# Attention scores in PSUM: one four-bank tile for two key tiles, in place of two double-bank tiles

## The chip, the cores and the metric

The kernel runs on one core of a Trainium2 chip. The metric is the device time of one execution in microseconds (us); the kernel before took 431.75 us (median of 3 runs, 431.55 to 432.01). The engines are TensorE (PE; its weight loads are PEld), VectorE (DVE), ScalarE (ACT), GpSimd (POOL) and SyncE (SP), which issues the DMAs.

## The reference, cut to what matters

```python
# q, k, v: (2, 12, 448, 64)
scores = q @ k.T / sqrt(64)
attn = softmax(cap * tanh(scores / cap))            # cap = 30
x = (attn @ v) as (2, 448, 768)
h = gelu(x @ w_in)                                  # 768 -> 1024
u, v = h[..., :512], h[..., 512:]
v = layernorm(v) * g_ln
x = x + (u * (w_sg @ v + b_sg)) @ w_out             # w_sg mixes the 448 positions
u = x + (relu(x.T @ w_tok1) @ w_tok2).T             # 448 -> 256 -> 448
out = u + relu(u @ w_ch1) @ w_ch2                   # 768 -> 1536 -> 768
```

Matrices other than the attention weights are split into a high and a low part (`hi`, `lo`), and a product is three matmuls: hi·hi, hi·lo, lo·hi.

## The kernel before, in words

Attention goes over 12 pairs of heads (`attention_all`). A pair has 448 keys: three key tiles of 128 (`j` = 0, 1, 2) with both heads, and a last tile that holds the 64 remaining keys of both heads. For each key tile PE writes the scores, keys by queries, into a PSUM tile `sc` of two banks, one bank per head (`scores`, matmuls of L574; the last tile `last`, L694, fills one bank). ACT takes the tanh from PSUM into an SBUF tile (L548) and then the exp in place (L556), both in `weigh`. The next step multiplies by the values (`values`, L611, four-byte floats, two records of the trace for each matmul; `rest_of`, L594, for the last key tile) into two banks `A` from the tag `gm`, and DVE normalises (`normalise`).

PSUM has eight banks: four single banks (`gm`) and two double banks (`sc`). `sc` also serves the transposes (`tr_unit`, L948) and the first layer of the channel MLP (`ch1_unit`). SBUF tiles come from tags with a fixed number of buffers (`BUFS`).

The order of work on each engine is written by a planner (`Plan.schedule`), not by hand. It takes the operations with estimated durations and keys, and each time it issues the operation that can start first on its engine; of those that can start at once, the one with the lowest key. A dependency between engines costs `LAT` = 140 ns in the plan. A buffer of a tag is handed out in the order of keys: an operation can only take one when all tiles of its tag with lower keys can have theirs too. The order that comes out is fixed; on the chip each engine works through its own list.

In step `n` the keys say: scores of key tiles 0 and 1 of pair `n` (key 10n, one PE operation of 12 matmuls; for `n` = 0 two operations of 6), the values of key tiles 0 and 1 of pair `n-1` (10n + 0.5, four operations of one matmul), scores of key tile 2 together with the rest of pair `n-1` (10n + 4), the last key tile (10n + 4.1), the values of key tile 2 of pair `n-1` (10n + 5, two operations). From the sixth pair on, matmuls of the first MLP for batch 0 (L305) are ready too and can lie between them. Beside the attention, weights are read, rebuilt from 8-byte floats and split: ACT L430, L441, L454; DVE L461, L472, L483; the split L382, L386, L398, L399. The query and key tiles of a pair are split too (tag `q`, DVE L398 for the low part).

After the attention: the first MLP of batch 1 (136 to 167 us), the mixing over positions `sg_unit` (to 185), `out_unit`, the transposes (202 to 224), `tok1_unit`, `tok2_unit` (234 to 249), `ch1_unit` (249 to 336) and `ch2_unit` (336 to 423).

Of the kernel before, what the change touches and what calls it, by code (L numbers as in the profile page):

```python
# [8 lines left out]
F32R = mybir.dt.float32r  # L9
# [235 lines left out]
class Net:  # L245
# [79 lines left out]
    def consts(self):  # L325
        nc, io = self.nc, self.io
        c = lambda name, shape, dt=F32: self.pool.tile(shape, dt, tag=name, name=name, bufs=1)
        cap = c("cap", [128, 1])
        self.acap = c("acap", [128, 1])
        self.qs = c("qs", [128, 1])  # L330
        self.guard = c("guard", [128, 1])
        self.cb = Buf("const", None, None)
        self.cb.ap = cap
        self.gb = Buf("const", None, None)
        self.gb.ap = self.guard
        self.load(512, lambda: nc.sync.dma_start(out=cap, in_=io["cap"]), [self.cb], key=-14.85)
# [32 lines left out]
        warm = self.bank2()  # L369
# [173 lines left out]
    def weigh(self, sc, nn, te, key, dt=0.2):  # L543

        nc = self.nc
        self.act(
            nn * S,
            lambda: nc.scalar.activation(te.ap, sc[:, 0:nn, :S], AF.Tanh, scale=self.qs),  # L548
            [sc, self.cb],
            [te],  # L550
            60,
            key,
        )
        self.last_exp = self.exps[int(key // 10)] = self.act(
            nn * S,
            lambda: nc.scalar.activation(te.ap, te.ap, AF.Exp, scale=self.acap),  # L556
            [te, self.cb],
            [te],
            190,
            key + dt,  # L560
        )

    def scores(self, qk, js, key, more=(), extra=0.0):

        nc = self.nc
        part, tiles = qk[:2]
        scs = [self.bank2() for _ in js]

        def fn():
            for sc, j in zip(scs, js):  # L570
# [9 lines left out]
        self.pe(  # L580
            3 * len(js) + 3.7 * len(more) + 0.5,
            fn,
            (tiles if js[0] else tiles[:2]) + [t for m in more for t in m[1]],
            scs + [t for m in more for t in m[2]],
            key,
        )
        return scs

    def rest_of(self, qk, E, A):


        def fn():
            for h, rows in enumerate((LO, UP)):
                self.nc.tensor.matmul(  # L594
                    A[h][:, :S],
                    qk[2][rows, 9:11].rearrange("p c d -> p (c d)"),
                    E[3][rows, 0],
                    start=False,
                    stop=False,
                )  # L600

        return fn, [qk[2], E[3]], A

    def values(self, qk, E, A, js, key):
        nc = self.nc
        V = qk[2]
        for j in js:
            for h in range(2):

                def av(j=j, h=h):  # L610
                    nc.tensor.matmul(  # L611
                        A[h][:, :S],
                        V[:, 3 * j + h : 3 * j + h + 2].rearrange("p c d -> p (c d)"),
                        E[j][:, h],
                        start=(j == 0),
                        stop=(j == 2),
                    )

                self.pe(3.7, av, [V, E[j]], [A[h]], key)

    def normalise(self, n, A):
        nc = self.nc
# [44 lines left out]
    def attention_all(self):  # L667
# [3 lines left out]
        for n in range(B * NP + 1):  # L671
            k0 = 10.0 * n
            if n < B * NP:
                qk = self.pair_in(n)
                E = {j: self.a([128, 2, S]) for j in range(3)}
                E[3] = self.h([128, 1, S])
                A = [self.bank() for _ in range(2)]
                for js in ([[0], [1]] if n == 0 else [[0, 1]]):
                    for i, (j, sc) in enumerate(zip(js, self.scores(qk, js, k0 + 0.3 * js[0]))):
                        self.weigh(sc, 2, E[j], k0 + 0.1 * j)  # L680
            if old:
                oqk, oE, oA = old
                self.values(oqk, oE, oA, [0, 1], k0 + 0.5)
                more = [self.rest_of(oqk, oE, oA)]
            if n < B * NP:
                (sc,) = self.scores(qk, [2], k0 + 4, more if old else ())
                self.weigh(sc, 2, E[2], k0 + 4)
                sc = self.bank2()

                def last(sc=sc, part=qk[0]):  # L690

                    ks, every = slice(KJ[3], KJ[3] + 128), slice(0, 128)
                    for t, (k, q) in enumerate(THREE):
                        nc.tensor.matmul(sc[:, 0, :S], part(k, every, ks), part(q, every, QC), start=(t == 0), stop=(t == 2))  # L694

                self.pe(3.5, last, qk[1], [sc], k0 + 4.1)
                self.weigh(sc, 1, E[3], k0 + 4.1)
            else:
                f, r, w = more[0]
                self.pe(4, f, r, w, k0 + 4)  # L700
# [1 line left out]
                self.values(oqk, oE, oA, [2], k0 + 5)  # L702
                xs.append(self.normalise(n - 1, oA))
            if n < B * NP:
                old = qk, E, A
        return xs

    def attention_anycap(self, n):
# [231 lines left out]
    def tr_unit(self, x2, s):  # L940

        nc = self.nc
        ps = self.bank2()
        cs = slice(0, 128) if s is None else slice(s * 128, (s + 1) * 128)

        def fn():
            for d in range(ND):
                nc.tensor.transpose(ps[:, d // 3, (d % 3) * 128 : (d % 3 + 1) * 128], x2[d][:, cs], self.ident)  # L948

        self.pe(3, fn, x2, [ps])  # L950
        t = [self.a([128, 2, 384], F32R) for _ in range(2)]
        src = lambda p=slice(0, 128): ps[p, :, 0:384]
        if s is None:
            self.halves(768, lambda b, p: t[b][p], src, [ps], t, True)
        else:
            hi, lo = t
            self.act(768, lambda: nc.scalar.copy(hi.ap, src()), [ps], [hi], 50)
            self.rest(768, lambda: lo.ap, src, lambda: hi.ap, [ps, hi], [lo], psum=True)
        return t

    def pack2(self, x2):
# [57 lines left out]


    def ch1_unit(self, ws, U, f):
        ps = self.bank2()
        for m, ts in enumerate(WIDE):
            terms = []
            for d in range(ND):
                n, c = divmod(f % 2 * ND + d, 4)
# [4 lines left out]
                    [ws[n], U[0][d], U[1][d]],  # L1031
                )
            size = ts.stop - ts.start
            self.mm(ps, lambda m=m, size=size: ps[:, m, :size], terms, size / S)
        hi, lo = (self.buf("q" if f < 3 else "a", [128, 2 * S], F32R) for _ in range(2))
        src = lambda: ps.ap.rearrange("p m n -> p (m n)")[:, : 2 * S]
        self.relu_split(2 * S, (hi, lambda: hi.ap), (lo, lambda: lo.ap), ps, src)
        return hi, lo

    def ch2_unit(self, ws, h2, U, d):  # L1040
        nc, io = self.nc, self.io
        for m, ts in enumerate(WIDE):
# [3 lines left out]
            for f in range(NC):  # L1046
                cs = slice(f % 4 * 128, (f % 4 + 1) * 128)
                terms += self.three(
                    lambda i, f=f, cs=cs: ws[f // 4][:, i, cs], lambda i, f=f, ts=ts: h2[f][i][:, ts], [ws[f // 4], *h2[f]]
                )  # L1050
            self.mm(ps, lambda ps=ps, size=size: ps[:, :size], terms, size / S)
            n = 2 if (m, d) == (1, ND - 1) else 1
# [187 lines left out]
```

## Time and profile before

| | |
|---|---|
| median of 3 runs | 431.75 us |
| the profiled execution | 431.57 us |
| its span, first to last instruction | 429.8 us |
| PE busy | 420.9 us (98%) |
| DVE busy | 259.0 us (60%) |
| ACT busy | 244.0 us (57%) |
| POOL busy | 87.0 us (20%) |
| mean granted TensorE clock | 0.997 |

The time of the profiled execution lies 1.8 us above its span: what comes before the first and after the last instruction. The table is an average over stages; which engine is short where stands in the view by stages.

### The profile page before, as it was taken

The numbers are of one execution on the slowest core, as the hardware profiler recorded it, in microseconds if no ns is written. First come the engines' busy times: TensorE is split into PE (matmuls) and PEld (weight loads), VectorE is DVE, ScalarE is ACT, GpSimd is POOL, SyncE is SP. The second block draws the span as 40 slices with busy tenths as digits, with TensorE's granted clock in tenths as the row PEclk, the third lists the DMA queues.
The fourth block names the chain that finished last, engine by engine and source line by source line (L and its number), as shares of the span: only waits on it lengthen the run. The fifth ranks groups of instructions, "written<-read, shape, count | busy, mean of one in ns | idle before, by whom it ended". The sixth has DMA issues, their size and how long they took to land.

```text
span 429.8 us, 5380 instructions
## 1 busy us (share of the span) xinstructions
PE 420.9 (98%) x2026; PEld 342.5 (80%) x2026; DVE 259.0 (60%) x417; ACT 244.0 (57%) x366; POOL 87.0 (20%) x90
## 2 busy tenths in 40 slices
PE   8999999999999999999999999999999999999993
PEld 5555556677665899999999989989898899889983
DVE  3699995878358777996556898565313143344210
ACT  5999788797957446535657817575514324353100
POOL 0223320010001333546004395001010011011100
PEclk9999999999999999999999999999999999999998
DMA  7735254564130102104302105425301323543111
GB/s 258 273 129 178 82 155 149 179 220 127 49 99 9 42 0 100 43 15 165 111 0 99 49 19 178 146 100 182 112 0 49 100 94 121 189 116 127 39 37 34
DMA packets 14866, 44.84 MB, mean 104 GB/s; under 512 B 1904, under 2 KB 3568, under 8 KB 14832
## 3 DMA queue, kind: packets, MB, share of 16 engines
q1 hardware_dynamic: 14688, 44.31, 31.2%
q8 instruction: 18, 0.29, 0.3%
q14 instruction: 16, 0.13, 0.1%
q10 hardware_dynamic: 144, 0.10, 0.1%
HBM read 41.65 MB, written 2.75 MB: 103 GB/s over the span
## 4 chain that ended last, share of the span: by engine, by line
PE 96%; ACT 2%; issue 0%; POOL 0%; DVE 0%; DVEq 0%; POOLq 0%
PE gm L305 52%; PE sc L305 20%; PE gm L611 12%; PE sc L574 6%; PE gm L594 2%; PE sc L694 2%; ACT a L548 1%; PE sc L948 1%; PE sc L373 1%; ACT a L556 1%; ACT h L556 0%; ACT r L430 0%; ACT h L548 0%; DVE h L1066 0%; POOL ident masks.py:199 0%
## 5 line engine op out<-in xcount | busy, mean ns | idle before, releaser
L305 PE MATMUL gm<-a,a 128*128 128x384 f32 (+2 forms) x556 | 113.1, 359 | 0.0
L305 PEld LDWEIGHTS gm<-a,a 128*128 128x128 f32 x556 | 100.6, 188 | 8.6
L305 PE MATMUL sc<-x,a 128*128 128x512 f32 (+1 forms) x432 | 87.3, 363 | 0.0
L305 PEld LDWEIGHTS sc<-x,a 128*128 128x128 f32 x432 | 78.3, 188 | 8.9
L611 PE MATMUL gm<-a,v 128*128 128x448 f32 x144 | 59.7, 548 | 0.4 <-ACT a L556 0.4
L461 DVE SCALAR_TENSOR_TENSOR t<-r,t 128x512 int32<-128x512 int32 (+1 forms) x52 | 39.6, 765 | 30.8 <-ACT t L454 27.5
L305 PE MATMUL gm<-q,a 128*128 128x448 f32 (+2 forms) x268 | 57.0, 366 | 0.0
L430 ACT ACTIVATE r<-r 128x512 f32<-128x512 f32 (+1 forms) x58 | 38.4, 664 | 29.5 <-DMA r<-ch_in 24.6
L441 ACT ACTIVATE t<-r 128x512 uint16<-128x512 uint16 (+1 forms) x52 | 40.5, 781 | 25.1 <-DVE a L398 23.6
L305 PEld LDWEIGHTS gm<-q,a 128*128 128x128 f32 x268 | 49.8, 188 | 4.9
L399 POOL TENSOR_TENSOR a<-t,a 128x512 fp32r<-128x512 f32 x18 | 24.5, 1362 | 118.7 <-DVE a L382 105.0
L611 PEld LDWEIGHTS gm<-a,v 128*128 128x128 f32 x144 | 26.2, 189 | 22.7 <-issue 19.5
L398 DVE TENSOR_TENSOR a<-t,a 128x512 fp32r<-128x512 f32 x38 | 29.2, 770 | 19.6 <-POOL a L386 18.7
L454 ACT ACTIVATE t<-r 128x512 f16<-128x512 f32 (+1 forms) x52 | 39.9, 769 | 0.0
L548 ACT ACTIVATE a<-sc,qs 128x896 f32<-128x896 f32 x36 | 35.0, 1004 | 7.8 <-PE sc L574 7.6
L386 POOL TENSOR_SCALAR a<-t 128x512 fp32r<-128x512 f32 x18 | 11.2, 620 | 127.2 <-PE gm L305 65.6
L556 ACT ACTIVATE a<-a,acap 128x896 f32<-128x896 f32 x36 | 36.4, 1038 | 0.0
L305 PE MATMUL gm<-x,a 128*128 128x448 f32 x144 | 31.5, 375 | 0.0
L305 PEld LDWEIGHTS gm<-x,a 128*128 128x128 f32 x144 | 27.1, 188 | 3.5 <-issue 1.5
L981 DVE SCALAR_TENSOR_TENSOR a<-sc,a 128x896 fp32r<-128x896 f32 x9 | 9.8, 1091 | 31.3 <-ACT a L978 31.3
L305 PE MATMUL gm<-a,x 128*128 128x512 f32 x108 | 26.5, 401 | 0.0
L978 ACT ACTIVATE a<-sc 128x896 fp32r<-128x896 f32 x9 | 8.3, 921 | 31.9 <-PE sc L305 31.9
(98 smaller groups left out, 452.0 us busy)
## 6 DMA issues: line engine op xcount, KB each, us to landing
r<-ch_in SPq DMA_DIRECT2D x36, 512.0 KB, 3.4
r<-w_in_in SPq DMA_DIRECT2D x12, 512.0 KB, 4.6
q<-qk_in SPq DMA_DIRECT2D x11, 480.0 KB, 4.3
v<-va_in SPq DMA_DIRECT2D x12, 352.0 KB, 4.1
r<-w_out_in SPq DMA_DIRECT2D x6, 512.0 KB, 3.4
out_t<-h SPq DMA_DIRECT2D x6, 256.0 KB, 2.0
r<-tok_in SPq DMA_DIRECT2D x2, 512.0 KB, 3.5
out_t<-h SPq DMA_DIRECT2D x5, 192.0 KB, 3.6
```

What stands on the lines that cost most here:

```text
L305: self.nc.tensor.matmul(view(), l, rr, start=(i + m == 0), stop=(i + m == n - 1))
L386: lambda: nc.gpsimd.tensor_scalar(out(), src(), 1.0, 0.0, ALU.mult, ALU.add),
L398: "DVE": ("DVE", n / 0.96 + 155, lambda: nc.vector.tensor_tensor(**args()), not psum),
L399: "POOL": ("POOL", n * 2.3 + 60, lambda: nc.gpsimd.tensor_tensor(**args()), True),
L430: lambda: nc.scalar.activation(raw[:, :, 1].bitcast(F32), raw[:, :, 1].bitcast(F32), AF.Copy, scale=2.0**-112),
L441: lambda: nc.scalar.activation(t.ap.bitcast(U16)[:, 0::2], raw.ap.rearrange("p n t -> p (n t)").bitcast(U16)[:, 1::4], AF.Copy, scale=2.0* ...
L454: lambda: nc.scalar.activation(t.ap.bitcast(F16)[:, 1::2], raw[:, :, 1].bitcast(F32), AF.Copy),
L461: lambda: nc.vector.scalar_tensor_tensor(out=t.ap, in0=raw[:, :, 1], scalar=3, in1=t.ap, op0=ALU.logical_shift_left, op1=ALU.bitwise_or),
L548: lambda: nc.scalar.activation(te.ap, sc[:, 0:nn, :S], AF.Tanh, scale=self.qs),
L556: lambda: nc.scalar.activation(te.ap, te.ap, AF.Exp, scale=self.acap),
L574: nc.tensor.matmul(sc[:, h, :S], part(k, rows, ks), part(q, rows, QC), start=(t == 0), stop=(t == 2))
L611: nc.tensor.matmul(A[h][:, :S], V[:, 3 * j + h : 3 * j + h + 2].rearrange("p c d -> p (c d)"), E[j][:, h], start=(j == 0), stop=(j == 2),)
```

## The change

The tag `sc` holds one tile of four banks. The scores of key tiles 0 and 1 of a pair go into it, one tanh covers both (1792 elements per partition), then one exp. Key tile 2 and the last key tile go into the same four banks afterwards (three banks used, 1344 elements), again with one tanh and one exp. The SBUF tiles for them have a tag of their own, `e`, with three buffers; `a` goes from 21 to 16 buffers and `h` from 13 to 12. The first pair has a form of its own (`first`): its first two key tiles go into the four `gm` banks, with one tanh for each head and one exp for each key tile. Of the transposes, units 0 and 2 of a batch use the four-bank tile, unit 1 and the remainder use two `gm` banks in two halves. `ch1_unit` uses `gm` banks, with a relu and a split for each half, and its results for `f` = 3, 4, 5 lie in `e`. In the plan, the fixed cost of a tanh goes from 60 to 230 ns and that of an exp from 190 to 270 ns. The last hunks of the diff are of `tr_unit` (unit 1 and the remainder) and of `ch1_unit`.

```diff
-BUFS = {"x": 6, "v": 3, "q": 6, "a": 21, "r": 2, "t": 3, "h": 13, "p": 6, "gm": 4, "sc": 2, "sm": 4}
+BUFS = {"x": 6, "v": 3, "q": 6, "e": 3, "a": 16, "r": 2, "t": 3, "h": 12, "p": 6, "gm": 4, "sc": 1, "sm": 4}
...
-    def bank2(self):
-        return self.buf("sc", [128, 2, 512])
+    def bank4(self):
+        return self.buf("sc", [128, 4, 512])
...
-        scs = [self.bank2() for _ in js]
+        sc = self.bank4()
...
-                            sc[:, h, :S], part(k, rows, ks), part(q, rows, QC), start=(t == 0), stop=(t == 2)
+                            sc[:, 2 * m + h, :S], part(k, rows, ks), part(q, rows, QC), start=(t == 0), stop=(t == 2)
...
+    def first(self, qk, e):
...
+        for j in range(2):
+            banks = [self.bank() for _ in range(2)]
...
+            self.pe(3, fn, tiles if j else tiles[:2], banks, 0.1 * j)
+            for h, ps in enumerate(banks):
+                self.act(
+                    S,
+                    lambda j=j, h=h, ps=ps: nc.scalar.activation(e[:, 2 * j + h], ps[:, :S], AF.Tanh, scale=self.qs),
...
+                    0.1 * j,
+                )
+            self.act(
+                2 * S,
+                lambda j=j: nc.scalar.activation(
+                    e[:, 2 * j : 2 * j + 2], e[:, 2 * j : 2 * j + 2], AF.Exp, scale=self.acap
+                ),
...
+                0.1 * j + 0.2,
+            )
...
-                E = {j: self.a([128, 2, S]) for j in range(3)}
-                E[3] = self.h([128, 1, S])
+                e01, e23 = self.buf("e", [128, 4, S]), self.buf("e", [128, 3, S])
                 A = [self.bank() for _ in range(2)]
-                for js in ([[0], [1]] if n == 0 else [[0, 1]]):
-                    for i, (j, sc) in enumerate(zip(js, self.scores(qk, js, k0 + 0.3 * js[0]))):
-                        self.weigh(sc, 2, E[j], k0 + 0.1 * j)
+                if n == 0:
+                    self.first(qk, e01)
+                else:
+                    self.weigh(self.scores(qk, [0, 1], k0), 4, e01, k0)
...
-                (sc,) = self.scores(qk, [2], k0 + 4, more if old else ())
-                self.weigh(sc, 2, E[2], k0 + 4)
-                sc = self.bank2()
+                sc = self.scores(qk, [2], k0 + 4, more if old else ())
...
-                        nc.tensor.matmul(sc[:, 0, :S], part(k, every, ks), part(q, every, QC), start=(t == 0), stop=(t == 2))
+                        nc.tensor.matmul(sc[:, 2, :S], part(k, every, ks), part(q, every, QC), start=(t == 0), stop=(t == 2))
...
-                self.weigh(sc, 1, E[3], k0 + 4.1)
+                self.weigh(sc, 3, e23, k0 + 4.1)
...
+        for m in range(2):
+            ps = self.bank()
...
+            self.pe(1.5, fn, x2[3 * m : 3 * m + 3], [ps])
...
-        ps = self.bank2()
+        if f in (3, 4, 5):
+            both = self.buf("e", [128, 2, 2 * S], F32R)
...
         for m, ts in enumerate(WIDE):
+            ps = self.bank()
```

## Rows read from the trace of the kernel before

**Rows 1.** The page, parts 1 and 4: busy time, and the chain's shares.
```profile
PE 420.9 (98%) x2026; PEld 342.5 (80%) x2026; DVE 259.0 (60%) x417; ACT 244.0 (57%) x366; POOL 87.0 (20%) x90
...
PE 96%; ACT 2%; issue 0%; POOL 0%; DVE 0%; DVEq 0%; POOLq 0%
```
**Rows 2.** Busy by stage: window; PE, PEld, DVE, ACT, POOL busy us; clock; DMA share, GB/s.
```profile
19.90:66.70 46.80, 46.31 (x210) 25.58 (x211) 45.64 (x76) 41.85 (x54) 12.53 (x12) 1.00 0.47 150
66.70:136.30 69.60, 69.60 (x304) 46.16 (x301) 44.52 (x85) 56.28 (x80) 4.04 (x4) 1.00 0.35 116
...
249.00:336.40 87.40, 87.40 (x435) 78.47 (x434) 46.31 (x57) 41.75 (x62) 19.75 (x17) 1.00 0.31 103
...
423.30:429.80 6.50, 0.00 (x0) 0.00 (x0) 0.61 (x2) 0.00 (x0) 0.00 (x0) 0.77 0.14 40
```
**Rows 3.** Waits of PE, 14 to 136 us: us in total, times, longest.
```profile
PE sc L574 <- ACT a L548: 0.5, 1, 0.5
```
**Rows 4.** ACT instructions by form: count, busy us, mean ns of one, idle before.
```profile
L556 ACT ACTIVATE a<-a,acap 128x896 f32<-128x896 f32 x36 | 36.4, 1038 | 0.0
L548 ACT ACTIVATE a<-sc,qs 128x896 f32<-128x896 f32 x36 | 35.0, 1004 | 7.8 <-PE sc L574 7.6
...
L556 ACT ACTIVATE h<-h,acap 128x448 f32<-128x448 f32 x12 | 8.0, 664 | 0.0
L548 ACT ACTIVATE h<-sc,qs 128x448 f32<-128x448 f32 x12 | 7.6, 634 | 2.3 <-PE sc L694 2.3
```
**Rows 5.** The chain that ended last, its start: start us, us, what.
```profile
6.23 1.02 ACT a L548
...
8.32 1.79 ACT a L548 x2
10.11 0.93 ACT a L556
11.04 0.53 ACT h L548
...
12.50 0.56 ACT h L556
13.05 0.55 ACT r L430
13.61 0.90 ACT a L548
...
14.55 0.87 PE sc L574 x6
...
16.97 3.01 PE gm L611 x8
19.97 1.43 PE sc L574 x12
```
**Rows 6.** PE in order of time, first 30 us: start, us, instruction.
```profile
21.33 1.77 PE L611 MATMUL gm<-a,v 128*128 128x448 f32 x4
```
**Rows 7.** PE in order of time, 30 to 140 us.
```profile
42.26 4.67 PE L611 MATMUL gm<-a,v 128*128 128x448 f32 x12
...
48.85 0.47 PE L574 MATMUL sc<-q 64*128 64x448 f32 x2 [0.49 <-ACT a L548]
...
56.39 1.02 PE L611 MATMUL gm<-a,v 128*128 128x448 f32 x2
```
**Rows 8.** DVE in order of time: the low parts of queries and keys of two pairs.
```profile
9.46 1.16 DVE L398 TENSOR_TENSOR q<-q,q 128x960 fp32r<-128x960 f32 x1
...
44.47 1.16 DVE L398 TENSOR_TENSOR q<-q,q 128x960 fp32r<-128x960 f32 x1
```
**Rows 9.** In order of time, 218 to 226 us: PE, then ACT, then DVE.
```profile
218.58 2.33 PE L305 MATMUL gm<-a,a 128*128 128x384 f32 x12
...
224.03 0.80 ACT L957 CAST a<-sc 128x768 fp32r<-128x768 f32 x1 [0.99 <-PE sc L948]
...
224.86 0.96 DVE L398 TENSOR_TENSOR a<-sc,a 128x768 fp32r<-128x768 f32 x1 [0.27 <-ACT a L957]
```

More of the change, by code (lines that the diff above doesn't have):

```diff
@@ L368, in consts @@
         self.big = c("big", [1, 1], I32)
-        warm = self.bank2()
+        warm = self.bank4()
         def spin():
@@ L550, in weigh @@
             [te],
-            60,
+            230,
             key,
@@ L558, in weigh @@
             [te],
-            190,
+            270,
             key + dt,
@@ L566, in scores @@
         part, tiles = qk[:2]
-        scs = [self.bank2() for _ in js]
+        sc = self.bank4()
         def fn():
-            for sc, j in zip(scs, js):
+            for m, j in enumerate(js):
                 ks = slice(KJ[j], KJ[j] + 128)
@@ L582, in scores, with fn @@
             fn,
-            (tiles if js[0] else tiles[:2]) + [t for m in more for t in m[1]],
-            scs + [t for m in more for t in m[2]],
-            key,
-        )
-        return scs
+            tiles + [t for m in more for t in m[1]],
+            [sc] + [t for m in more for t in m[2]],
+            key,
+        )
+        return sc
+    def first(self, qk, e):
+        nc = self.nc
+        part, tiles = qk[:2]
+        for j in range(2):
+            banks = [self.bank() for _ in range(2)]
+            def fn(j=j, banks=banks):
+                ks = slice(KJ[j], KJ[j] + 128)
+                for t, (k, q) in enumerate(THREE):
+                    for ps, rows in zip(banks, (LO, UP)):
+                        nc.tensor.matmul(ps[:, :S], part(k, rows, ks), part(q, rows, QC), start=(t == 0), stop=(t == 2))
+            self.pe(3, fn, tiles if j else tiles[:2], banks, 0.1 * j)
[3 more added lines that the diff above has]
+                    lambda j=j, h=h, ps=ps: nc.scalar.activation(e[:, 2 * j + h], ps[:, :S], AF.Tanh, scale=self.qs),
+                    [ps, self.cb],
+                    [e],
+                    230,
+                    0.1 * j,
[5 more added lines that the diff above has]
+                ),
+                [e, self.cb],
+                [e],
+                270,
+                0.1 * j + 0.2,
+            )
     def rest_of(self, qk, E, A):
@@ L596, in fn @@
                     qk[2][rows, 9:11].rearrange("p c d -> p (c d)"),
-                    E[3][rows, 0],
+                    E[1][rows, 2],
                     start=False,
@@ L600, in fn @@
                 )
-        return fn, [qk[2], E[3]], A
+        return fn, [qk[2], E[1]], A
     def values(self, qk, E, A, js, key):
@@ L613, in av @@
                         V[:, 3 * j + h : 3 * j + h + 2].rearrange("p c d -> p (c d)"),
-                        E[j][:, h],
+                        E[j // 2][:, j % 2 * 2 + h],
                         start=(j == 0),
@@ L617, in av @@
                     )
-                self.pe(3.7, av, [V, E[j]], [A[h]], key)
+                self.pe(3.7, av, [V, E[j // 2]], [A[h]], key)
     def normalise(self, n, A):
@@ L704, in attention_all @@
             if n < B * NP:
-                old = qk, E, A
+                old = qk, (e01, e23), A
         return xs
@@ L942, in tr_unit, with all_six, fn @@
         nc = self.nc
-        ps = self.bank2()
         cs = slice(0, 128) if s is None else slice(s * 128, (s + 1) * 128)
[L946 to L950, printed above, removed]
         t = [self.a([128, 2, 384], F32R) for _ in range(2)]
[L952 to L955, printed above, removed]
+        if s in (0, 2):
             hi, lo = t
-            self.act(768, lambda: nc.scalar.copy(hi.ap, src()), [ps], [hi], 50)
-            self.rest(768, lambda: lo.ap, src, lambda: hi.ap, [ps, hi], [lo], psum=True)
+            ps = self.bank4()
+            def all_six():
+                for d in range(ND):
+                    nc.tensor.transpose(ps[:, d // 3, (d % 3) * 128 : (d % 3 + 1) * 128], x2[d][:, cs], self.ident)
+            self.pe(3, all_six, x2, [ps])
+            self.act(768, lambda: nc.scalar.copy(hi.ap, ps[:, 0:2, 0:384]), [ps], [hi], 230)
+            self.rest(768, lambda: lo.ap, lambda: ps[:, 0:2, 0:384], lambda: hi.ap, [ps, hi], [lo], psum=True)
+            return t
+        for m in range(2):
+            ps = self.bank()
+            def fn(m=m, ps=ps):
+                for d in range(3):
+                    nc.tensor.transpose(ps[:, d * 128 : (d + 1) * 128], x2[3 * m + d][:, cs], self.ident)
+            self.pe(1.5, fn, x2[3 * m : 3 * m + 3], [ps])
+            src = lambda p=slice(0, 128), ps=ps: ps[p, 0:384]
+            if s is None:
+                self.halves(384, lambda b, p, m=m: t[b][p, m], src, [ps], t, True)
+            else:
+                hi, lo = t
+                self.act(384, lambda m=m, src=src: nc.scalar.copy(hi[:, m], src()), [ps], [hi], 50)
+                self.rest(384, lambda m=m: lo[:, m], src, lambda m=m: hi[:, m], [ps, hi], [lo], psum=True)
         return t
@@ L1021, in ch1_unit @@
     def ch1_unit(self, ws, U, f):
-        ps = self.bank2()
+        if f in (3, 4, 5):
+            both = self.buf("e", [128, 2, 2 * S], F32R)
+            hi = lo = both
+            view = lambda i: both[:, i]
+        else:
+            hi, lo = pair = [self.buf("q" if f < 3 else "a", [128, 2 * S], F32R) for _ in range(2)]
+            view = lambda i: pair[i].ap
         for m, ts in enumerate(WIDE):
+            ps = self.bank()
             terms = []
@@ L1033, in ch1_unit @@
             size = ts.stop - ts.start
[L1034 to L1038, printed above, removed]
+            self.mm(ps, lambda ps=ps, size=size: ps[:, :size], terms, size / S)
+            self.relu_split(
+                size,
+                (hi, lambda ts=ts: view(0)[:, ts]),
+                (lo, lambda ts=ts: view(1)[:, ts]),
+                ps,
+                lambda ps=ps, size=size: ps[:, :size],
+            )
+        return hi, lo, view
     def ch2_unit(self, ws, h2, U, d):
```

2 lines of the change are left out of this document (1 added, 1 removed).

## The prediction

> **What bounds the kernel now.** First the page's busy times and the chain of waits [rows 1]: PE is busy for 98% of the span and the chain lies on PE for 96%. So only PE's own work, or time in which PE has none, can move the end. The PE work itself is left alone by the change: as many matmuls of the same shapes. Then the stages [rows 2]: from 19.9 to 66.7 us PE, DVE (45.64 of 46.80 us) and ACT (41.85) are all nearly full. It is the stretch where PE has only attention to do, with no matmul of the first MLP beside it. After it ACT falls to 56.28 of 69.60 us and PE stays full. Then PE's waits: from 14 us to the end of the attention one wait of 0.5 us on a tanh [rows 3]. What a shorter ACT can give back is therefore small: that wait, and holes before 14.55 us, where the chain runs over ACT [rows 5]. The idle end of 6.5 us [rows 2] is the output's way out and stays.
>
> **ACT's instructions.** A tanh of 896 elements takes 1004 ns, of 448 takes 634; an exp 1038 and 664 [rows 4]. So 448 elements cost 370 and 374 ns, and a tanh of 1792 should take 1.74 us, of 1344 1.37; an exp 1.79 and 1.41. Started one behind the other they lie closer: tanh 0.90 for 896 (1.79 for two) and 0.53 for 448, exp 0.93 and 0.56 [rows 5]. A pair now takes 3 x (0.90 + 0.93) + 0.53 + 0.56 = 6.58 us of ACT. With 0.37 for each 448, the large ones take 1.63 + 1.67 + 1.27 + 1.30 = 5.87 us: 0.7 us less for each of 11 pairs, 7.8 us in all. On PE's path this is worth nothing by itself, since PE is already covered.
>
> ACT is 89% busy from 19.9 to 66.7 us [rows 2], and still PE waited once for it [rows 3]. The Trainium skill, "Perfetto Trace Analysis", section Optimizing Scalar/DVE Operations, says that larger operations help a saturated engine, but that where ScalarE is not saturated and makes bubbles on others, breaking instructions up lets work complete sooner. The trace agrees with neither half alone, as ACT is nearly full and yet PE is the bound; by the second half the change goes the wrong way and the sum would be that of the first rival.
>
> **The start.** Now PE gets to the third key tile of pair 1 at 14.55 us [rows 5], and from there it is fed. By then it has done all scores of pair 0, its values of key tiles 0 and 1, and scores 0 and 1 of pair 1; after the change the same work stands before that point, so the point itself measures the shift. The single tile makes a chain: tanh of pair 0's second tile, scores 0 and 1 of pair 1 (1.43 us [rows 5]), their tanh (1.74), then the third key tile. Pair 1's low parts are there at 9.46 + 1.16 = 10.62 us [rows 8], too early to matter. Two orders of ACT are near a tie in the plan.
> (a) All four small tanhs first: from 6.23 us, 4 x 0.53 = 8.35; two exps, 10.21; the tanh of 1344 ends at 11.58. PE is then in the middle of the values of key tile 1 (two matmuls of 0.75, from 3.01 for eight records [rows 5]) and starts pair 1's scores between 11.65 and 12.45. They end at 13.1 to 13.95, the tanh at 14.9 to 15.7. So PE goes on at 15.0 to 15.75: 0.45 to 1.2 us later.
> (b) The exp of key tile 0 between: 6.23 + 0.53 + 0.63 = 7.39, its end 8.4, two tanhs to 9.4, tanh of 1344 to 10.8, scores to 12.25; exps of tile 1 and of the second tile occupy ACT until 12.9, tanh to 14.65: 0.1 us later. A weight's 0.55 us on ACT, which stands at 13.05 now [rows 5], can fall in front in either order.
> I take +0.5 us, between the two. The ends are +1.2 and -0.6: if the tanh of 1344 went ahead of both exps it would end at 9.9, the scores would run from 10.7, their tanh to 13.9, and PE would go on at 13.95.
>
> **The middle.** In `sc` there is now a closed loop for each pair: scores 0 and 1 (1.43), tanh (1.74), third key tile, rest and last tile (2.42, from 14.55 to 16.97 [rows 5]), tanh (1.37): 6.96 us and four handovers, under PE's own work of 8.35 (1.43 + 2.42 + six value matmuls of 0.75). So the loop fits, if value matmuls lie in the right places: 1.74 + 0.1 us of them behind scores 0 and 1, which is five records of 0.376, and 1.5 us behind the last tile. Before, the second bank pair was free after 0.90 us, and the trace shows what the planner put there: four records (1.77 us with the pipeline's run-in and end, 1.5 net) at 21.33 [rows 6] and once more in the same way at 38.3, none at 48 us, two at 56.39 [rows 7], six or more elsewhere before 66.7 us. At 48 us all twelve records had gone in front (42.26 [rows 7]), since the low parts of that pair were done only at 44.47 + 1.16 = 45.6 us [rows 8] on a DVE that is full. There PE waited 0.49 us [rows 7]; with one tanh over both tiles it waits 1.85, that is 1.35 more. The other three places are short by 0.35, 0.35 and 1.1 us, if the order stays. All together +3.15 us at most. The planner counts a tanh of 1792 as 1.72 us and can keep value matmuls back where it has any, and ACT is freer; at best the 0.5 us goes as well, -0.5. I take +0.7, half of the one place where the matmuls had run out for certain. After 66.7 us matmuls of the first MLP fill such holes (PE is 69.60 of 69.60 busy [rows 2]): nothing.
>
> **Fewer `a` buffers.** At the transposes, two weights and the tiles of seven transposed units (14) filled 16 of 21 buffers, and the five left over took the first results of `tok1_unit`. With 16, the third unit of batch 1 and the second half of the first results must wait until batch 0 has been read. Then a cast (0.80 us) and a subtraction (0.96 [rows 9]) follow, some 2.0 us with handovers, while PE still has two operations of six matmuls (12 take 2.33 with run-in and end [rows 9]). +0.2 us, from -0.2 to 2.0. In `ch1_unit` ACT and DVE do two small instructions for one large, but are busy 41.75 and 46.31 of 87.40 us [rows 2]: nothing while PE is full, and if that cover were gone, for each of 12 units some 0.16 us, what is left of a tanh's 0.90 without its two times 0.37. The halves of the transposes add nothing if they stay side by side.
>
> **The sum.** 431.57 us (the profiled execution, 1.77 us more than its span) + 0.5 + 0.7 + 0.2 = 432.97. The median of the runs stands 0.18 above that execution: 433.1; rounded, 433.0 us.
>
> **The rivals.**
> *The single tile stalls every short handover* (slower). PE waits after scores 0 and 1 at all four places: +3.15 with +1.2 at the start and +0.2 makes 431.75 + 4.5 = 436.3; it decides when fewer than five value records lie behind scores 0 and 1. For it: the four short places, and DVE, which sends the query tiles late. Against: the planner is told the new length. I hold its full size for one in ten; smaller parts of it are in the forecast.
> *Holes cancel* (no change). The wait at 48 us goes, the start loses 0.5, the rest is nothing: 431.75 + 0.0 to 0.5. For it: PE has value matmuls for 4.5 us in each pair and needs cover for 1.84 + 1.5 only. Against: they were spent in front at 42.26 [rows 7].
> *ACT's 7.8 us reach PE* (faster). A freer ACT takes casts from a full DVE, the queries come earlier, and the start runs by the early tile: -0.6 at the start and -0.5 in the middle, 431.75 - 1.1 = 430.65. For it: ACT and DVE are both nearly full until 66.7 us. Against: PE hardly waits for them, so 1.1 us is about all there is. It decides if pair 1's scores start before 11.3 us.
>
> **How the numbers follow.** This kernel's measurement tells 0.2%, 0.86 us, from no change. Slower by more than that (the forecast and the first rival, 432.6 and above): 0.44, of which 0.10 is the rival. No change (holes cancel): 0.33. Faster: 0.23. The likeliest's own range is 432.6 to 434.6. The range is 430.7 to 435.2: below it lies about one tenth, where the start gains more than I see, and above it the first rival's full size.
>
> **What would show it.** Right: ACT's share from 20 to 66 us falls; the first group of scores of key tile 2 of pair 1 starts between 14.65 and 15.75 us; PE's waits on L548 add up to 1 to 2 us from 14 us to the end of the attention, at places with fewer than five value records behind scores 0 and 1; the stages from 136 us on are as long as before within 0.5 us. Wrong: PE's waits on the tanh gone, and scores of pair 1 before 11.3 us (faster); or PE waiting at most pairs; or a new wait around the transposes of more than 1 us, from the smaller tag `a`.

## The result and the profile after

The changed kernel takes 435.56 us (median of 4 runs, 435.43 to 436.51) against 431.65 for the kernel before: a ratio of 1.0102, 95% interval [1.009, 1.0113]. It is slower, as forecast, but by more: 433.0 was predicted, with 435.2 as the upper end. A second series of the same kernel gave 436.01 us (435.50 to 437.02), ratio 1.0108 [1.0093, 1.0123]. The profiled execution of after took 436.51 us, that of before 431.57. Of the four runs of after it was the slowest, so the profiles lie 4.9 us apart where the medians lie 3.9 apart.

First the page of after, its parts 1 and 4, and the busy times by stage (columns as in [rows 2]).

```profile
PE 422.9 (97%) x2026; PEld 342.4 (79%) x2026; DVE 260.4 (60%) x439; ACT 240.3 (55%) x337; POOL 84.5 (19%) x85
...
PE 88%; DVE 6%; ACT 3%; issue 1%; POOL 0%; DVEq 0%; ACTq 0%; POOLq 0%
```
```profile
7.30:14.55 7.25, 5.66 (x22) 3.26 (x21) 4.31 (x6) 7.25 (x8) 0.00 (x0) 0.78 0.98 373
...
19.90:66.70 46.80, 45.75 (x203) 24.76 (x202) 44.12 (x76) 36.89 (x31) 13.15 (x12) 1.00 0.44 135
66.70:136.30 69.60, 69.60 (x306) 46.50 (x306) 43.12 (x84) 54.50 (x60) 2.61 (x3) 1.00 0.39 127
...
249.00:336.40 87.40, 86.75 (x427) 77.14 (x427) 53.36 (x79) 48.64 (x81) 23.74 (x19) 1.00 0.34 115
```

PE's chain share falls from 96 to 88% [rows 1], and DVE comes onto the chain. ACT did get shorter from 19.9 to 66.7 us: 36.89 us in place of 41.85 [rows 2]. PE, the bound, has more holes in the same stretch. And the granted clock (the share of TensorE's full clock that it was given) is 0.78 from 7.30 to 14.55 us; before it was 1.00 there:

```profile
7.30:14.55 7.25, 6.78 (x30) 3.28 (x30) 3.39 (x5) 7.25 (x10) 0.00 (x0) 1.00 0.98 373
```

The instructions themselves came out as estimated. ACT by form (columns as in [rows 4]):

```profile
L556 ACT ACTIVATE e<-e,acap 128x1792 f32<-128x1792 f32 x11 | 19.7, 1790 | 0.3
L548 ACT ACTIVATE e<-sc,qs 128x1792 f32<-128x1792 f32 x11 | 19.3, 1753 | 9.2 <-PE sc L574 9.2
L556 ACT ACTIVATE e<-e,acap 128x1344 f32<-128x1344 f32 x12 | 17.0, 1414 | 0.2
L548 ACT ACTIVATE e<-sc,qs 128x1344 f32<-128x1344 f32 x12 | 16.5, 1378 | 11.3 <-PE sc L726 11.1
```

So the loss is not in ACT's instructions, but in when PE gets its work. The start times of PE's instructions cut the execution into stretches. The table has their lengths in us, of the profiled executions; the first column counts from the start of the span, each other one from the end of the column before it:

| kernel | to scores of key tile 2, pair 1 | to end of attention | to first transposes | to `tok2_unit` | to `ch1_unit` | to `ch2_unit` | to PE's end |
|---|---|---|---|---|---|---|---|
| before | 14.55 | 121.27 | 66.17 | 32.25 | 14.88 | 87.17 | 86.96 |
| after | 16.07 | 122.09 | 66.63 | 33.07 | 14.87 | 88.30 | 86.96 |
| difference | +1.5 | +0.8 | +0.5 | +0.8 | 0 | +1.1 | 0 |

These make 4.75 us at PE's end (423.25 to 428.00). Behind the first column the lengths repeat well: in kernels with the same code for a stretch they agree within 0.2 us (the attention takes 122.07 to 122.10 us in after, a_again, a_h1, a_wout and a_spin). The first column varies more: where the start is that of the kernel before (before, b_hold5, b_banks, b_keep) it is 14.05 to 14.55. Five places show in the trace of after.

*The start.* PE in order of time, then ACT (L606 is the tanh of one head in `first`):

```profile
7.30 0.88 PE L726 MATMUL sc<-a,a 128*128 128x448 f32 x3
9.76 0.47 PE L574 MATMUL sc<-q 64*128 64x448 f32 x2 [1.59 <-ACT e L548]
...
11.17 4.97 PE L645 MATMUL gm<-e,v 128*128 128x448 f32 x8
16.07 0.47 PE L574 MATMUL sc<-q 64*128 64x448 f32 x2
```
```profile
7.82 0.61 ACT L606 ACTIVATE e<-gm,qs 128x448 f32<-128x448 f32 x1
8.34 1.37 ACT L548 ACTIVATE e<-sc,qs 128x1344 f32<-128x1344 f32 x1
9.60 0.63 ACT L606 ACTIVATE e<-gm,qs 128x448 f32<-128x448 f32 x1
```

PE has nothing between the last key tile of pair 0 and the scores of pair 1. Then eight value records take 4.97 us, where eight take 3.27 in a_spin below: the first five start about 0.75 us apart, the others 0.38. So five run at the lower of the clock's two levels, 1.2 GHz.

*The middle.* PE's waits from 14 to 136 us, and the value records around one of them:

```profile
PE sc L574 <- ACT e L548: 0.9, 1, 0.9
```
```profile
35.30 3.92 PE L645 MATMUL gm<-e,v 128*128 128x448 f32 x10
...
40.57 1.02 PE L645 MATMUL gm<-e,v 128*128 128x448 f32 x2
42.49 0.47 PE L574 MATMUL sc<-q 64*128 64x448 f32 x2 [0.90 <-ACT e L548]
...
57.75 1.77 PE L645 MATMUL gm<-e,v 128*128 128x448 f32 x4
```

Ten records lie in front of the scores of key tiles 0 and 1, two behind, and the tanh of 1.75 us outlasts them. Four records, at 57.75, are nearly enough: the next scores start at 59.67, 0.15 us after their end. From the third key tile of pair 1 to the end of the attention PE is idle for 1.05 us, before for 0.49.

*The last `w_out` weights.* Near 200 us, before the first transposes, the weight loads wait for the low part of a weight:

```profile
200.15 0.91 PEld L305 LDWEIGHTS gm<-a,a 128*128 128x128 f32 x5 [0.49 <-DVE a L398]
```

*The transposes.* At 222.93 PE waits for DVE: the third unit of batch 1 needs the four-bank tile back from the first, whose low part DVE does only after two pieces of the remainder.

```profile
222.93 0.88 PE L983 MATMUL sc<-ident,h 128*128 128x128 f32 x6 [0.26 <-DVE a L398]
```
```profile
220.14 1.14 DVE L398 TENSOR_TENSOR a<-gm,a 64x384 fp32r<-64x384 f32 x2 [0.21 <-ACT a L381]
221.92 0.96 DVE L398 TENSOR_TENSOR a<-sc,a 128x768 fp32r<-128x768 f32 x1 [0.64 <-ACT a L986]
```

This wait is 0.26 of the 0.8 us. PE is idle for 0.36 us in the stretch from 204.79 to 237.87, before for 0; the rest lies inside its busy time.

*`ch1_unit`.* DVE in order of time, after and then before. L1060 of after is L1015 of before: the last sums of `tok2_unit`. L398 with `x` is the low part that `ch1_unit` reads.

```profile
252.24 4.14 DVE L398 TENSOR_TENSOR x<-h,x 128x448 fp32r<-128x448 f32 x4
256.31 0.61 DVE L1060 TENSOR_TENSOR h<-gm,h 128x448 f32<-128x448 f32 x1
256.84 1.24 DVE L461 SCALAR_TENSOR_TENSOR t<-r,t 128x512 int32<-128x512 int32 x1
258.01 1.43 DVE L398 TENSOR_TENSOR x<-h,x 128x448 fp32r<-128x448 f32 x1
```
```profile
250.26 1.14 DVE L1015 TENSOR_TENSOR h<-gm,h 128x448 f32<-128x448 f32 x2
251.50 2.80 DVE L398 TENSOR_TENSOR x<-h,x 128x448 fp32r<-128x448 f32 x2
254.22 3.20 DVE L461 SCALAR_TENSOR_TENSOR t<-r,t 128x512 int32<-128x512 int32 x2
```

Before, the last low parts are done at 254.30 us, and the weight's L461 comes behind them. After, the last sum lies behind four low parts, a weight's L461 lies in front of the last low part, and that ends at 259.44 us, 6.7 us after `ch1_unit` began (before 5.2). PE waits for it:

```profile
259.49 2.70 PE L305 MATMUL gm<-x,a 128*128 128x512 f32 x12 [0.65 <-DVE x L398]
```

### The profile page after: what moved, and what is told of

It reads as the page before. It is cut to its first block, busy times and chain, and to the rows that moved or that the text cites. A ratio compares the mean times of both kernels' runs of the same rounds, so it can differ in the third digit from the quotient of the medians.

```text
span 434.7 us, 5383 instructions
## 1 busy us (share of the span) xinstructions
PE 422.9 (97%) x2026; PEld 342.4 (79%) x2026; DVE 260.4 (60%) x439; ACT 240.3 (55%) x337; POOL 84.5 (19%) x85
## 4 chain that ended last, share of the span: by engine, by line
PE 88%; DVE 6%; ACT 3%; issue 1%; POOL 0%; DVEq 0%; ACTq 0%; POOLq 0%
PE gm L305 64%; PE gm L645 13%; PE sc L574 6%; PE gm L628 2%; PE sc L726 2%; DVE a L398 2%; DVE h L943 2%; DVE x L398 1%; ACT e L548 1%; ACT a L381 1%; DVE t L461 1%; PE sc L373 1%; PE sc L983 1%; DVE h L937 0%; ACT e L606 0%
## 5 line engine op out<-in xcount | busy, mean ns | idle before, releaser
L305 PE MATMUL gm<-x,a 128*128 128x512 f32 (+2 forms) x576 | 118.8, 366 | 0.6 <-DVE x L398 0.6
L305 PEld LDWEIGHTS gm<-x,a 128*128 128x128 f32 x576 | 105.2, 188 | 13.4 <-DVE x L398 1.4
L305 PE MATMUL gm<-a,a 128*128 128x384 f32 (+2 forms) x448 | 91.6, 359 | 0.2
L305 PEld LDWEIGHTS gm<-a,a 128*128 128x128 f32 x448 | 81.0, 188 | 7.3 <-DVE a L398 0.8
L645 PE MATMUL gm<-e,v 128*128 128x448 f32 x144 | 60.8, 561 | 0.0
L461 DVE SCALAR_TENSOR_TENSOR t<-r,t 128x512 int32<-128x512 int32 (+1 forms) x52 | 38.8, 746 | 34.6 <-ACT t L454 32.6
L548 ACT ACTIVATE e<-sc,qs 128x1344 f32<-128x1344 f32 (+1 forms) x23 | 35.8, 1558 | 20.5 <-PE sc L726 11.1
L645 PEld LDWEIGHTS gm<-e,v 128*128 128x128 f32 x144 | 27.0, 194 | 23.6 <-issue 21.8
L398 DVE TENSOR_TENSOR a<-t,a 128x512 fp32r<-128x512 f32 x41 | 30.0, 733 | 21.8 <-POOL a L386 18.4
L556 ACT ACTIVATE e<-e,acap 128x1344 f32<-128x1344 f32 (+1 forms) x23 | 36.7, 1594 | 0.5
L1026 DVE SCALAR_TENSOR_TENSOR a<-gm,a 128x384 fp32r<-128x384 f32 (+1 forms) x20 | 11.8, 596 | 21.8 <-ACT a L1023 19.1
L305 PEld LDWEIGHTS gm<-a,x 128*128 128x128 f32 x108 | 20.3, 188 | 5.5 <-issue 1.3
```

Source lines behind the costliest of these rows:

```text
L305: self.nc.tensor.matmul(view(), l, rr, start=(i + m == 0), stop=(i + m == n - 1))
L398: "DVE": ("DVE", n / 0.96 + 155, lambda: nc.vector.tensor_tensor(**args()), not psum),
L461: lambda: nc.vector.scalar_tensor_tensor(out=t.ap, in0=raw[:, :, 1], scalar=3, in1=t.ap, op0=ALU.logical_shift_left, op1=ALU.bitwise_or),
L645: nc.tensor.matmul(A[h][:, :S], V[:, 3 * j + h : 3 * j + h + 2].rearrange("p c d -> p (c d)"), E[j // 2][:, j % 2 * 2 + h], start=(j == 0) ...
L1026: lambda: nc.vector.scalar_tensor_tensor(out=lo[1](), in0=src(), scalar=0.0, in1=hi[1]().bitcast(F32), op0=ALU.max, op1=ALU.subtract),
```

## The experiments

All are compared with runs of the kernel before on the same chip; stretches are those of the table above. The two series of the changed kernel lie 0.45 us apart, and the gains of single edits in the medians are 0.5 to 0.8 us, so which part of the loss an edit removes is read from the stretches. "Four edits" are those of `a_best`.

**a_spin: PE busy in the hole at the start.**
```diff
+                    o = self.plan.op([("PE", 8 * 213, turn, False, 0)], 5.0, [], [idle])
+                    o.deps.append(done)
```


> The changed kernel, with eight 128-column matmuls on the identity put into PE's hole between the last key tile of pair 0 and the scores of pair 1 (8.0 to 9.8 us in the changed kernel); their result is not used. Theory 1 (the hole itself is harmless for what follows; what costs is that TensorE's clock falls to its lower level, since the five value records from 11.2 us take 747 ns in place of 376): with PE busy in the hole these records take 0.38 us, the scores of key tile 2 of pair 1 start near 14.7 us in place of 16.1, and the time falls by about 1.4 us. Theory 2 (the start is late because of the chain tanh - scores - tanh through the single tile, whatever the clock): still at 16.1 us, the time unchanged or longer.

434.97 us (434.77 to 435.20), ratio 1.0084 [1.007, 1.0097]. PE in order of time:

```profile
8.17 1.95 PE L735 MATMUL gm<-ident 128*128 128x128 f32 x16
10.04 0.47 PE L574 MATMUL sc<-q 64*128 64x448 f32 x2
...
11.46 3.27 PE L645 MATMUL gm<-e,v 128*128 128x448 f32 x8
14.77 0.47 PE L574 MATMUL sc<-q 64*128 64x448 f32 x2
```

The eight value records are back at 3.27 us, and the third key tile starts at 14.77 in place of 16.07. Theory 1 holds at that place: with useless work in the hole the clock stays at 1.00 (7.30 to 14.55 us) and the delay goes. In the medians the gain is 0.6 us (in the ratios 0.8), half of what was expected. One reason is under a_again: the clock falls in some executions of after and not in others.

**a_free: the first pair's values may start behind their own exp.**
```diff
+                    halves = [Half(e01, slice(2 * j, 2 * j + 2)) for j in range(2)]
+                    E[:2] = [(t, 0) for t in halves]
+                    self.first(qk, halves)
```


> The changed kernel, where for the first pair the plan sees the two key tiles of the four-tile SBUF buffer as two buffers, so that the values of key tile 0 can be planned behind the exp of key tile 0 and not behind that of key tile 1. Theory 1: the two value matmuls fall into the hole at 8 us, the clock stays at 2.4 GHz, the scores of key tile 2 of pair 1 start at 14.7 to 15.0 us in place of 16.1 and the time falls by 1.1 to 1.4 us. Theory 2 (chain through the single tile): they start at 16 us and the time stays within 0.3 us of the changed kernel's.

434.94 us (434.53 to 435.18), ratio 1.0081 [1.0067, 1.0095], 0.6 us under the changed kernel. PE in order of time:

```profile
8.67 1.67 PE L651 MATMUL gm<-e,v 128*128 128x448 f32 x4
...
13.06 1.77 PE L651 MATMUL gm<-e,v 128*128 128x448 f32 x4 [1.26 <-ACT e L622]
```

The values of key tile 0 move into the hole (from 8.67 us), the granted clock is 1.00 from 7.30 to 14.55, and the third key tile starts at 15.27, 0.8 us earlier than in after; expected were 1.1 to 1.4. A new wait of 1.26 us on the exp of key tile 1 takes a part back. So the hole comes from the plan: it knows the four-tile SBUF buffer as one, and puts the first values behind the last exp into it.

**b_hold5: the kernel before with five `a` buffers fewer after the attention.**
```diff
+        held = [self.a([128, 8]) for _ in range(5)]
+        for t in held:
+            self.gps(100, lambda t=t: nc.gpsimd.memset(t.ap, 0.0), [x[1][ND - 1]], [t], 133.5)
...
+        for t in held:
+            self.gps(100, lambda t=t: nc.gpsimd.memset(t.ap, 0.0), [U[1][ND - 1]], [t])
```


> The kernel before, with five of the 21 buffers of tag a taken away from the end of the attention until the last tile of tok2_unit is there (a small memset at each end on POOL). Theory A (the 2.4 us that the changed kernel loses between the attention and ch2_unit come from the smaller tag a: weights of w_out and ch1 and the results of tok1_unit wait for buffers): 1.0 to 2.4 us slower than before, the losses at the last w_out weights (185 to 202 us), at the transposes and tok1_unit (202 to 237 us) and in the first units of ch1_unit. Theory B (they come from the banks: transposes and ch1_unit share the four single banks): no slower than 0.3 us.

433.13 us (432.66 to 434.06), ratio 1.0047 [1.0033, 1.006]. Theory A holds for two of the three places: +0.5 us to the first transposes (66.67 for 66.17) and +1.8 in `ch1_unit` (88.94 for 87.17, where after has 88.30). DVE has the order of after there:

```profile
252.56 0.61 DVE L1015 TENSOR_TENSOR h<-gm,h 128x448 f32<-128x448 f32 x1
253.09 1.25 DVE L461 SCALAR_TENSOR_TENSOR t<-r,t 128x512 int32<-128x512 int32 x1
254.26 1.43 DVE L398 TENSOR_TENSOR x<-h,x 128x448 fp32r<-128x448 f32 x1
```

But PE's wait falls at another place than in after:

```profile
265.17 3.02 PE L305 MATMUL sc<-x,a 128*128 128x512 f32 x12 [1.04 <-DVE q L981]
```

DVE L981 is the split of a result of `ch1_unit`, and DVE came to it only after a row of operations for weights. So the missing buffers delay `ch1_unit` through DVE's queue in both kernels, by different operations.

At the transposes and `tok1_unit` nothing is lost (32.12 for 32.25): that part was a miss of theory A.

**b_banks: the kernel before with the single banks of after.** Units 1 and the remainder of `tr_unit`, and `ch1_unit`, take the form of the changed kernel.
```diff
         for m, ts in enumerate(WIDE):
+            ps = self.bank()
```


> The kernel before, with the transposes of unit 1 and of the remainder, and ch1_unit, put into single banks in halves as in the changed kernel; the attention, the double banks for units 0 and 2 and all buffer counts as before. Theory A (buffers of tag a): within 0.3 us of before. Theory B (banks): 1.0 to 2.4 us slower, with waits of PE at the transposes and in the first units of ch1_unit.

432.11 us (431.73 to 432.48), ratio 1.0019 [1.001, 1.0028]: between the two theories. +0.3 us to `tok2_unit` (32.54), +0.4 in `ch1_unit` (87.56).

**a_h1: three of the four results of `tok1_unit` in the idle `e` buffers.**
```diff
+            both = self.buf("e", [128, 2, 2, 384], F32R)
+            hi, lo = Half(both, 0), Half(both, 1)
```


> The changed kernel, with three of the four results of tok1_unit (high and low part together) in the three buffers of tag e, which lie idle at that time, in place of tag a. Theory A (too few a buffers: the weights of ch1 get their buffers only when tok1_unit is done, and their DVE work lands between the last tiles of tok2_unit): the losses from the first transposes to tok2_unit (0.8 us) and in ch1_unit (1.1 us) go, the wait before the last out_unit (0.4 us near 200 us) stays; 1.5 to 2.0 us faster than the changed kernel. Theory B (the single banks that ch1_unit and the transposes now share with tok2_unit): both stay, within 0.3 us of the changed kernel.

434.80 us (433.93 to 436.06), ratio 1.0071 [1.0059, 1.0084]; 0.8 us under the changed kernel's first series (1.3 by the ratios), where 1.5 to 2.0 were expected. `ch1_unit` goes from 88.30 to 87.55 us, to what b_banks has, and DVE does all low parts before the weight's L461 (here L469), as before:

```profile
253.82 4.96 DVE L406 TENSOR_TENSOR x<-h,x 128x448 fp32r<-128x448 f32 x4
258.70 3.20 DVE L469 SCALAR_TENSOR_TENSOR t<-r,t 128x512 int32<-128x512 int32 x2
```

The transposes and `tok1_unit` stay at 33.07: the half of theory A that spoke of them fell.

**a_wout: three `w_out` weights in `e`.**
```diff
-        wout = [self.weight(io["w_out"][d], 512, wk("wout", k, d), "wout") for d in range(ND)]
+        wout = [self.weight(io["w_out"][d], 512, wk("wout", k, d), "wout", None, "e" if d > 2 else None) for d in range(ND)]
```


> The changed kernel, with the last three of the six w_out weights in the buffers of tag e in place of tag a. Theory A (too few a buffers): PE's wait near 200 us (0.4 us between the end of the attention and the first transposes) goes, the losses at tok1_unit and in ch1_unit stay; 0.3 to 0.6 us faster than the changed kernel. Theory B (banks): no difference at any of the three places.

435.05 us (433.83 to 436.45), ratio 1.0079 [1.0061, 1.0098]; 0.5 us under the changed kernel (1.0 by the ratios), expected were 0.3 to 0.6. To the first transposes 66.16 us, as before, and PE is never idle from 185 us on to there: the wait near 200 us was for a `w_out` weight that had no buffer. To `tok2_unit` 32.47, 0.6 us less than in after, and PE's wait for DVE at the transposes is gone; that was not expected.

**a_keep: values kept back behind the next scores.**
```diff
+                if 1 < n < 8:
+                    for o in made[-3:]:
+                        o.deps.append(wrote)
```


> The changed kernel, where for pairs 2 to 7 the last three of the four value operations of key tiles 0 and 1 must be planned behind the scores of the next pair, so that six value records (2.3 us) always lie behind these scores. Theory M1 (PE waits in the attention because the value matmuls are used up in front of the scores, and the tanh over both tiles takes 1.75 us): the waits of 0.97 us at 42.5 us and of 0.2 us at 59.7 us go; the end of the attention comes 0.6 to 1.2 us earlier than in the changed kernel, and the time falls by as much. Theory M2 (the low parts of the queries come late from DVE, and PE would wait for them in any order): PE waits in front of the scores instead, no gain.

434.78 us (433.92 to 436.20), ratio 1.008 [1.0065, 1.0096]; 0.8 us under the changed kernel, expected were 0.6 to 1.2. The attention takes 121.05 us from the third key tile on, in place of 122.09, and no wait of PE is left between 14 and 136 us. M1 holds: the large tanh costs nothing when six value records lie behind the scores. This profiled execution had the same hole at the start (1.47 us), yet the clock stayed at 1.00 and the values took 3.27 us:

```profile
9.98 0.47 PE L574 MATMUL sc<-q 64*128 64x448 f32 x2 [1.47 <-ACT e L548]
...
11.54 3.27 PE L645 MATMUL gm<-e,v 128*128 128x448 f32 x8
14.94 0.47 PE L574 MATMUL sc<-q 64*128 64x448 f32 x2
```

**a_best: all four edits** (a_spin, a_h1, a_wout, a_keep).

> The changed kernel with all four edits together: eight matmuls in PE's hole at 8 us, three results of tok1_unit and three w_out weights in tag e, and the value operations kept behind the scores. If the three causes (clock at the start, value matmuls used up in the attention, buffers of tag a later) make up the whole loss, it is 3.3 to 4.3 us faster than the changed kernel, that is 431.2 to 432.2 us, level with the kernel before. If a part of the loss is due to the single four-bank tile itself, more than 1 us stays.

432.75 us (432.35 to 433.09), ratio 1.0024 [1.0014, 1.0034]. It is 2.8 us under the first series of after (3.4 by the ratios), and 1.1 us stay, a little more than was allowed for; by the stretches of the profiled execution 0.4 lie between the first transposes and `tok2_unit` and 0.4 in `ch1_unit` (87.54). The start takes 0.7 us more than in before (15.24) and the attention 0.3 less.

**a_best_sc: `ch1_unit` takes the four-bank tile for every second unit.**
```diff
+        quad = None if f % 2 else self.bank4()
...
+            ps = quad or self.bank()
```


> The changed kernel with the four edits as before, and in ch1_unit every second unit (f even) in the four-bank tile in place of two single banks. Theory: the 0.37 us that are left in ch1_unit (0.39 us in the kernel before with single banks there) come from waiting for single banks that tok2_unit still holds; they go, and it is 0.3 to 0.5 us faster than the version with four edits (432.75 us), that is 432.3 us. Rival: they come from the smaller, more numerous relu and split instructions; no gain.

431.92 us (431.21 to 432.45), ratio 1.0017 [1.0008, 1.0026]. `ch1_unit` takes 86.97 us, 0.2 less than before: the rest there was a matter of banks, not of the smaller instructions, of which there are as many. In the profiled execution, the fastest of its series, PE ends at 423.29 us, before at 423.25; the medians still differ by 0.5 us (0.7 by the ratios). The smaller tag `h` and the new costs of tanh and exp in the plan were not tried alone. They are part of this kernel too, and it comes within 0.5 us of the kernel before.

**b_keep: the kernel before with two value operations kept back.**
```diff
+                    for o in made[-2:]:
+                        o.deps.append(wrote)
```


> The kernel before, where for pairs 2 to 7 the last two of the four value operations of key tiles 0 and 1 are planned behind the scores of the next pair. If PE's one wait of 0.49 us on a tanh there has the same cause as those of the changed kernel (no value matmuls left behind the scores), it goes, and the time falls by 0.3 to 0.7 us, to about 431.0 us. If the wait is due to late query tiles, nothing is gained.

431.23 us (430.22 to 431.64), ratio 0.9991 [0.9982, 1.0000]. The one wait in the attention of before goes (121.02 for 121.27); 0.3 to 0.7 us were expected, and the gain in the time, 0.2 us, is at the edge of what can be measured. Without waits the attention takes the same time with two large tanhs (a_keep, 121.05) as with the smaller ones.

**a_again: the changed kernel once more.**

> The changed kernel once more, unchanged, on the same chip and beside the same runs of the kernel before. If TensorE's clock falls behind the hole at 8 us in some executions only, its times spread over more than 1 us, between about 434.5 and 436.5 us, while those of the version with PE busy in the hole (434.77 to 435.20 us) did not; if the clock always falls, they lie within 0.5 us around 435.6.

435.50 to 437.02 us in 4 runs, clock 0.78 from 7.30 to 14.55 us in the profiled one. The spread is 1.5 us, a_spin's 0.4. With a_keep's execution, where the clock stayed up behind the same hole, this says that it falls in some executions and not in others. The mean granted clock of whole runs agrees. It is 0.992 in the four profiled executions with the fall and 0.995 or more in all others. Of the eight runs of after and a_again, four have 0.992 or 0.993 and took 435.64 to 437.02 us; the other four have 0.995 or 0.996 and took 435.43 to 435.79. All ten runs of a_spin and a_free have 0.995 or more. So the medians of after mix both kinds, and an edit that keeps the clock up gains less in the median than in the profiles. What decides whether it falls, no run here shows.

## Why the prediction was wrong

The forecast added 1.4 us to the profiled execution before (with the median's 0.18 that makes 433.15, which was set down as 433.0); the profiled one after has 4.9 more, the medians 3.9. Two terms of the sum failed, the start and, worst, what the fewer buffers and banks cost after the attention. Of the signs, ACT's share fell as said, but the stages from 136 us on are 2.4 us longer where "within 0.5 us" was forecast, the scores of key tile 2 of pair 1 start at 16.07 us, outside 14.65 to 15.75, and PE's waits on L548 make 0.9 us, just short of 1 to 2.

**The bound and the instructions: right.** PE stayed the bound, and 5 us less of ACT in its fullest stretch gave PE nothing. The tanh of 1792 and 1344 elements take 1.753 and 1.378 us (estimated 1.74 and 1.37), the exps 1.790 and 1.414 (1.79 and 1.41).

**The start: +1.5 in place of +0.5 us.** The step that failed is the sentence in order (a) by which PE "is then in the middle of the values of key tile 1" when the tanh of 1344 is done. Neither order (a) nor (b) came about as written: ACT put that tanh between the two small tanhs of key tile 1, it ended at 9.71 us, and pair 1's scores began at 9.76, earlier than in any of my cases. By the rule of my third rival (scores before 11.3 us) that should have been faster. It was not, because the values of key tile 0, which I had running from its own exp, were planned behind the exp of key tile 1: the four tiles are one buffer to the planner. PE stood idle for 1.59 us and the clock fell. a_spin and a_free each remove this. With a full clock the third key tile starts at 14.75 to 15.27 us (a_spin, a_free, a_keep, a_best, a_best_sc), 0.2 to 0.7 us later than in before, about what I had forecast for all of it; with the fall at 16.07 to 16.67 (after, a_again, a_h1, a_wout). A hole in PE's work was priced at its length. That the clock may go down behind it was in none of the cases.

**The middle: +0.8, forecast +0.7.** The mechanism is right: value matmuls spent in front of the scores, then a tanh over both tiles that outlasts what is left behind them (1.75 us, where 0.90 us freed the second bank pair before). It happened at 41 us, with two records behind, and hardly at 58, with four. a_keep shows it by taking it away. That the size fits is in part luck: 0.7 was half of the loss at the pair of 48 us, and in the changed kernel that pair has six records behind its scores and no wait; another pair has one.

**After the attention: +2.4 in place of +0.2 us, the term that was worst; at least 1.2 of it are the fewer `a` buffers.** The step that failed is the one that looked at one place, the transposes and `tok1_unit`, where PE has other work, and asked only whether its own tiles come in time. The shortage passes on to whoever is next in the tag's order of keys. The w_out weights were late (+0.5; a_wout removes it, b_hold5 makes it). The ch1 weights' DVE work landed between the last low parts of `tok2_unit` (0.75 of the 1.1 us in `ch1_unit`; a_h1 removes it). That these weights got their buffers late is my reading of the plan; b_hold5 makes the same order on DVE and a larger loss (1.8 us), though PE waits there on another operation. The shortage alone, in the kernel before, costs 1.7 us.

**Costed at nothing: the banks.** `ch1_unit` in single banks costs 0.4 us and the transposes in halves 0.3 (b_banks). The sentence "nothing while PE is full" counted the instructions' cost and not how many banks `ch1_unit` has; a_best_sc, with more banks and as many instructions, has no loss left in `ch1_unit`. That the missing banks are those that `tok2_unit` still holds was my expectation there; no run separates it. Of the 0.8 us at the transposes, the other 0.5 went when the `w_out` weights lay in `e` (a_wout), but b_hold5, short of buffers in the same way, does not lose it. So it needs both changes, or another order than either gives; this stays open.

**The rivals.** The first, at 436.3 us, comes nearest to the time, for a reason that did not happen: it had PE stall at four handovers for 3.15 us, and the attention lost 0.8. The rule of the Trainium skill that I put beside it ("Perfetto Trace Analysis", Optimizing Scalar/DVE Operations: where ScalarE is not full and makes bubbles on others, breaking instructions up can let work finish sooner) pointed to the right wait, the 0.90 us of PE on a tanh, but a_keep removes that wait with the instructions as large as they are. The third rival's condition came true (scores of pair 1 before 11.3 us), and its time did not. *Holes cancel* is what a_keep's order would have given in the attention: its wait is gone and the stretch is 0.2 us shorter than in before.

## What to carry to other kernels

When an edit shrinks a shared pool of buffers, follow the pool's order past the stage in question: the price comes up where the next user's work lands, here stages later and on another engine's queue. When tiles are merged, ask what the scheduler now takes for one: everything that could start on the first part waits for the last. A hole in front of matmuls can cost more than its length if the clock goes down behind it; filling it with useless matmuls tells, and since the clock falls in some executions only, compare several runs and their granted clocks.

## What the runs showed of the hardware that was not expected

Behind a hole of 1.56 to 1.59 us on PE, matmuls ran at the lower clock level in the profiled executions of after, a_again, a_h1 and a_wout (granted clock 0.76 to 0.78 from 7.30 to 14.55 us). In after it met five value records, 0.75 us each for 0.38; in the other three, part of the scores in front of them and some of the value records. From the first scores of pair 1 to its third key tile PE took 6.2 to 6.8 us in these four, and 4.7 to 5.0 in a_spin, a_keep, a_best and a_best_sc, where the clock stayed at 1.00. In a_keep the hole was nearly as long, 1.47 us; in a_free a wait of 1.26 us left the clock at 1.00 as well. The kernel before, whose waits there are of 0.2 us, has 1.00 in the same window. So the clock can fall behind a hole of 1.6 us, and where the limit lies these runs do not show.
